# Ten ssm_k blocks in the head, their writes on GpSimd behind the gathers, weights ahead of them, bfloat16 one-hots

## The chip, the cores and the metric

The kernel runs on one core of a Trainium2 chip. The metric is the device time of one execution in microseconds; the median of several runs is quoted. TensorE is called PE (its weight loads PEld), VectorE DVE, ScalarE ACT, GpSimd POOL and SyncE SP. A DMA is issued on the queue of an engine: SP, ACT or POOL.

## The reference

Two branches work on the same tokens, `x = A_q` of 2048 rows by 512 columns, and a gate mixes them:

```python
g = _sigmoid((x * gate_w).sum(-1, keepdims=True))
a = _A_ref(x, A_k, A_v, A_shift_k, A_ssm_k, A_ssm_D, B_x, ...)   # abridged
b = _B_ref(x, B_w_router, B_w_gate, B_w_up, B_w_down)
return g * a + (1 - g) * b
```

`a` is a short causal convolution of k (4 taps), times v, then a long causal convolution along the 2048 tokens with `ssm_k` (an FFT per channel in the reference), times q. `b` is a mixture of 8 experts: the router's logits choose two experts for each token, each expert is `(silu(x Wg) * (x Wu)) Wd` with 1376 hidden columns, and the softmax of the two logits weighs them.

## The kernel before

**The stream.** The experts are worked through one after the other, the fullest first. Expert r takes up to 568 rows, gathered from DRAM by an index list. Every matmul of an expert is done in three passes over split numbers (a high part, names ending in h, and a low part, ending in l), so that a weight tile `raw` gives `gh` (ACT) and `gl` (DVE), a down weight `rd` gives `dh` and `dl`, and the transposed tokens give `xh` (ACT) and `xl` (DVE). For one weight tile ft and one half h of the rows, `product(ft, h, u)` makes g (u = 0) and then u (u = 1) in PSUM banks of the tag "gu", of which there are three in turn; ACT's silu of g (`sg`) frees a bank, and so does DVE's multiplication of `sg` by u. The first half are token tiles 0 and 1, the second half tiles 2 to 4.

**The fill.** The long convolution is a transform in two stages. Stage 1 of `ssm_k` treats 16 blocks: a block is loaded (`k_load`, tile `kr`), PE multiplies it by a constant (`stage1_f32`, two matmuls of 512 columns in float32), the result is moved from PSUM to SBUF and written to the DRAM tensor `kd` (`out1`). Six blocks (`SEQ_N`), ks1 to ks6, are done in the head, ahead of expert 0. The other ten are generators that are stepped between the products of the experts (`tick`), as are the later stages of the convolution.

**The head.** Up to `order.close()` the order of every engine is the order of the program text: the tokens are read transposed, the router's logits, the ranks, the counts per expert, then for the first expert the index list: one-hots `hots` on DVE, small matmuls `list` on PE, `idf` and `gidx` on DVE, and five gathers `xg` on POOL. The number of the first expert, `eor0`, has to be read by SP before it can load that expert's weights. Each gathered tile is transposed on PE (`xgp`), giving `xh` and `xl`. `busy` issues matmuls with no use for their result. After the head a scheduler orders the rest.

**Buffers.** Pairs of blocks lie in tiles of 1024 columns: the tag "B" has 5 of them, "ev" has 3; "A" has 6 tiles of 512 columns. A tile given out again waits for the last reader of the one before it in that place.

Of the kernel before, what the change touches and what calls it, by code (L numbers as in the profile page):

```python
# [11 lines left out]
F32 = mybir.dt.float32  # L12
# [44 lines left out]
SEQ_N = 6  # L57
BUSY = (14, 3, 4, 1, 10, 6, 6)
# [77 lines left out]
def gated_mix(ctx: ExitStack, tc: tile.TileContext, a, out):  # L136
# [113 lines left out]
    def out1(p, dst, pl, name, later=False):  # L250
# [25 lines left out]
    def stage1_f32(x, dst, pl, name, later=False):  # L276
        if ordered and pl % 2 == 0:
            p = [turned(f"{name}p{t}") for t in range(2)]
        else:
            both = banks(f"{name}p")  # L280
            p = [half(both, t) for t in range(2)]
# [8 lines left out]
        out1(p if ordered else both, dst, pl, name, later)  # L290
# [22 lines left out]
    def k_out(pl, later=False):  # L313
        stage1_f32(kr[pl], kd, pl, f"ks{pl}", later)
# [180 lines left out]
    def ticks(n):  # L495
        for _ in range(n):
            tick()

# [4 lines left out]
    def expert(r):  # L503
# [12 lines left out]
        def load(ft, eng=sync):  # L516
# [4 lines left out]
            if r == 0 and ft in QN and not ordered:  # L521
                with after("act 0"):
                    act.dma_start(raw[:, :n], src)
# [4 lines left out]
            st["raw", ft] = raw[:, :n]  # L528

# [13 lines left out]
        def product(ft, h, u, hi_first=False):  # L543
# [13 lines left out]
            for kt in range(KT):  # L557
                last = mm3(p[:fw, :nn], ghv[:, u, kt], glv[:, u, kt], xh[:, kt, sl], xl[:, kt, sl],
                           start=(kt == 0), stop=(kt == KT - 1))
            return last  # L560

        def load_down(ft, eng=sync):
# [3 lines left out]
            if r == 0 and ft in QR and not ordered:  # L566
                with after("act 0"):
                    act.dma_start(rd[:fw], src)
            else:
                eng.dma_start(rd[:fw], src)  # L570
            st["rd", ft] = rd

# [130 lines left out]
    sums = rp.tile([P, 4, P], BF16, name="sums")  # L703
    pool.memset(sums[:, 2], 1.0)
# [14 lines left out]
    sync.dma_start(late, a["c_small"][:, P:NLATE])  # L719
    k_load(k_order[3])  # L720
    k_load(k_order[4])
    with after("sp"):
        pool.dma_start(cr, a["c_r"])
    sync.dma_start(c2, a["c_r2"])

# [61 lines left out]
    k_out(k_order[0])  # L787
    k_load(k_order[5])
    k_out(k_order[1])
# [7 lines left out]
    k_out(k_order[2])  # L797
    k_out(k_order[3])
# [14 lines left out]
    dve.tensor_tensor(oh0, key, top.to_broadcast([P, E]), op=ALU.is_equal)  # L813
    s0 = rp.tile([P, PL], F32, name="s0")
    n0 = rp.tile([P, PL], F32, name="n0")
    u0 = rp.tile([P, PL], F32, name="u0")
    e0 = rp.tile([P, E], F32, name="e0")
    ef0 = rp.tile([P, 1], F32, name="ef0")
    g5 = rp.tile([P, PL, TILES], F32, name="g5")
    dve.tensor_mul(w0, w0, oh0.unsqueeze(2).to_broadcast([P, E, PL]))  # L820
    dve.tensor_mul(e0, oh0, io8)
    dve.tensor_reduce(s0, w0.rearrange("p e a -> p a e"), op=ALU.add, axis=AX.X)
    dve.tensor_reduce(ef0, e0, op=ALU.add, axis=AX.X)
    s5 = [P, PL, TILES]
    dve.tensor_tensor(g5, s0.unsqueeze(2).to_broadcast(s5), thr[:, :TILES].unsqueeze(1).to_broadcast(s5), op=ALU.is_gt)
    dve.tensor_copy(eor0, ef0)
# [62 lines left out]
    k_out(k_order[4])  # L889
    act.activation(G, L9[:, :, E], AF.Exp, scale=-1.0)  # L890
    first.split(0, act)
    busy(none, BUSY[2])
    for i in range(0, PL, 4):
        dve.tensor_tensor(hot[:, i:i + 4], u0[:, i:i + 4].unsqueeze(2).to_broadcast([P, 4, P]),
                          io128n.unsqueeze(1).to_broadcast([P, 4, P]), op=ALU.is_equal)
        for j in range(i, i + 4):
            pe.matmul(pv0, hot[:, j], val0[:, j], start=(j == 0), stop=(j == PL - 1))
        if i + 4 < PL:
            busy(none, BUSY[3])
    read(0, pv0)  # L900
    k_out(k_order[5], later=True)
# [7 lines left out]
    act.activation(z, z, AF.Exp)  # L909
    rows0 = gather(0)  # L910
    next(rows0)
# [257 lines left out]
```

## Time and profile before

| | us |
|---|---|
| median of 3 runs | 965.4 (963.39 to 966.9) |
| the profiled execution | 962.82 |
| its span, first to last instruction | 960.9 |
| PE busy in the span | 941.3 (98%) |
| DVE busy | 619.4 (64%) |
| ACT busy | 538.2 (56%) |
| POOL busy | 139.6 (15%) |

The profiled execution is 1.9 us longer than its span, and lies 2.6 us below the median. An instruction's row gives its start and its duration; rows overlap a little, since the engines are pipelined, so the distance of two starts is the better price of one in a row of many. The bracket at a row's end is the time in which the engine had nothing to do before it, and what ended that.

### The profile page before, as it was taken

The numbers are of one execution on the slowest core, as the hardware profiler recorded it, in microseconds if no ns is written. First come the engines' busy times: TensorE is split into PE (matmuls) and PEld (weight loads), VectorE is DVE, ScalarE is ACT, GpSimd is POOL, SyncE is SP. The second block draws the span as 40 slices with busy tenths as digits, with TensorE's granted clock in tenths as the row PEclk, the third lists the DMA queues.
The fourth block names the chain that finished last, engine by engine and source line by source line (L and its number), as shares of the span: only waits on it lengthen the run. The fifth ranks groups of instructions, "written<-read, shape, count | busy, mean of one in ns | idle before, by whom it ended". The sixth has DMA issues, their size and how long they took to land. (4 is left out here: it accounts for less than half of the span.)

```text
span 960.9 us, 18311 instructions
## 1 busy us (share of the span) xinstructions
PE 941.3 (98%) x7079; PEld 832.4 (87%) x7079; DVE 619.4 (64%) x1160; ACT 538.2 (56%) x881; POOL 139.6 (15%) x125
## 2 busy tenths in 40 slices
PE   8799999999999999999999999999999999999996
PEld 3589999999999999888889898888888887888895
DVE  4597689889999454745656555664676655554541
ACT  3453344454646645678667877677776672334330
POOL 1202011300103020031100301003120301020002
PEclk9899999999999999999999999999999999999998
DMA  8875875644657445474434754457453849875413
GB/s 299 308 265 195 302 244 179 174 149 168 220 179 197 145 135 187 146 183 167 143 129 161 179 170 152 128 169 182 164 165 113 207 143 315 268 197 143 116 31 44
DMA packets 78827, 171.93 MB, mean 179 GB/s; under 512 B 8625, under 2 KB 9521, under 8 KB 78610
## 3 DMA queue, kind: packets, MB, share of 16 engines
q1 hardware_dynamic: 55330, 122.57, 38.7%
q0 software_dynamic: 10976, 23.78, 12.1%
q10 hardware_dynamic: 12432, 24.38, 6.8%
q8 instruction: 57, 0.93, 0.4%
q14 instruction: 32, 0.26, 0.1%
HBM read 127.13 MB, written 43.57 MB: 178 GB/s over the span
## 5 line engine op out<-in xcount | busy, mean ns | idle before, releaser
L197 PE MATMUL g<-xh,gh 128*128 128x256 f32 (+15 forms) x700 | 202.7, 290 | 1.0 <-DVE sg L589 1.0
L197 PE MATMUL u<-xh,gh 128*128 128x256 f32 (+14 forms) x704 | 202.0, 287 | 0.7 <-ACT sg L588 0.6
L198 PE MATMUL u<-xl,gh 128*128 128x256 f32 (+14 forms) x704 | 201.6, 286 | 0.0
L199 PE MATMUL u<-xh,gl 128*128 128x256 f32 (+14 forms) x704 | 201.3, 286 | 0.0
L198 PE MATMUL g<-xl,gh 128*128 128x256 f32 (+15 forms) x700 | 200.1, 286 | 0.0
L199 PE MATMUL g<-xh,gl 128*128 128x256 f32 (+15 forms) x700 | 200.1, 286 | 0.0
L197 PEld LDWEIGHTS g<-xh,gh 128*128 128x128 f32 (+1 forms) x700 | 130.2, 186 | 16.9 <-issue 9.6
L197 PEld LDWEIGHTS u<-xh,gh 128*128 128x128 f32 (+1 forms) x704 | 130.9, 186 | 7.4 <-issue 4.0
L589 DVE TENSOR_TENSOR sg<-sg,u 128x256 f32<-128x256 f32 (+14 forms) x176 | 74.7, 425 | 95.8 <-PE u L199 84.9
L199 PEld LDWEIGHTS u<-xh,gl 128*128 128x128 f32 (+1 forms) x704 | 131.0, 186 | 5.7 <-issue 5.7
L590 ACT ACTIVATE hh<-sg 128x256 fp32r<-128x256 f32 (+14 forms) x176 | 73.5, 419 | 111.2 <-DVE sg L589 110.9
L198 PEld LDWEIGHTS u<-xl,gh 128*128 128x128 f32 (+1 forms) x704 | 131.0, 186 | 5.3 <-issue 4.9
L199 PEld LDWEIGHTS g<-xh,gl 128*128 128x128 f32 (+1 forms) x700 | 130.3, 186 | 5.9 <-issue 5.7
L198 PEld LDWEIGHTS g<-xl,gh 128*128 128x128 f32 (+1 forms) x700 | 130.2, 186 | 5.0 <-issue 3.2
L197 PE MATMUL yp<-hh,dh 128*128 128x264 f32 (+12 forms) x440 | 127.2, 291 | 0.0
L198 PE MATMUL yp<-hl,dh 128*128 128x264 f32 (+12 forms) x440 | 126.6, 289 | 0.0
L199 PE MATMUL yp<-hh,dl 128*128 128x264 f32 (+12 forms) x440 | 126.4, 289 | 0.0
L541 DVE TENSOR_TENSOR gl<-raw,gh 128x1024 fp32r<-128x1024 f32 (+2 forms) x89 | 105.4, 1184 | 22.9 <-ACT gh L535 22.2
L535 ACT ACTIVATE gh<-raw 128x1024 fp32r<-128x1024 f32 (+1 forms) x88 | 91.2, 1036 | 42.4 <-PE u L198 31.1
L588 ACT ACTIVATE sg<-g 128x256 f32<-128x256 f32 (+14 forms) x176 | 67.4, 386 | 80.8 <-PE g L199 72.2
L597 ACT ACTIVATE dh<-rd 128x512 fp32r<-128x512 f32 (+1 forms) x88 | 53.3, 627 | 70.5 <-DMA rd<-in_wd 30.6
L460 POOL DMA_INDIRECT xg<-in_q,gidx x37 | 44.7, 1207 | 325.8 <-PE xgp L469 288.7
(286 smaller groups left out, 1614.3 us busy)
## 6 DMA issues: line engine op xcount, KB each, us to landing
raw<-in_wgu SPq DMA_DIRECT2D x78, 512.0 KB
rd<-in_wd SPq DMA_DIRECT2D x77, 256.0 KB
kl<-kd SPq DMA_DIRECT2D x16, 512.0 KB
xl<-xd SPq DMA_DIRECT2D x32, 256.0 KB
zd<-ze ACTq DMA_DIRECT2D x16, 512.0 KB
zl<-zd SPq DMA_DIRECT2D x16, 512.0 KB
out<-zt SPq DMA_DIRECT2D x21, 256.0 KB
krow<-in_kpad SPq DMA_DIRECT2D x19, 256.0 KB
```

The source lines that it names most:

```text
L197: pe.matmul(p, wh, hi, start=start, stop=False)
L198: pe.matmul(p, wh, lo, start=False, stop=False)
L199: return pe.matmul(p, wl, hi, start=False, stop=stop)
L460: anchor["pool"] = pool.indirect_dma_start(out=xg[:w], out_offset=None, in_=a["q"], in_offset=bass.IndirectOffsetOnAxis(ap=gidx[:w, col:co ...
L535: act.activation(st["gh", ft], raw, AF.Copy)
L541: dve.tensor_sub(st["gl", ft][:, c], raw[:, c], st["gh", ft][:, c].bitcast(F32))
L588: act.activation(sg[:fw, :nn], pp[0][:fw, :nn], AF.Silu)
L589: dve.tensor_mul(sg[:fw, :nn], sg[:fw, :nn], pp[1][:fw, :nn])
L590: act.activation(hh[:fw, sl], sg[:fw, :nn], AF.Copy)
L597: act.activation(dh[:fw], rd[:fw], AF.Copy)
```

## The change

The head now does ten blocks of stage 1 (`SEQ_N` 10) and the stream six. All ten are loaded at the program's start, right behind the tokens and constants, and fill the five "B" places. Nothing is written to `kd` until the gathers have been issued: the writes are collected in `written` and then issued on POOL, behind the five gathers, as 13 DMAs. So the results stay in SBUF: ks1, ks3 and ks5 in "A", ks2, ks4, ks6, ks8 and ks10 in "ev", ks7 and ks9 in "B". Since "ev" has three places, ks8 takes the place of ks2, and ks10 that of ks4, when those have been written. Four of the results are moved out of PSUM later than their matmuls (`hold`), ks7, ks8 and ks10 by DVE. The last two gathered tiles move from "A" to places of the transposed tokens.

The one-hots are made from bfloat16 operands, with the four compared tokens innermost, against a table `io4` that POOL makes. The three steps from `oh0` to `eor0` go from DVE to POOL, as five. The silu table is loaded earlier on ACT, `busy` runs less, and the loads of raw2, rd0 and rd1 on ACT's queue come later.

```diff
-SEQ_N = 6
-BUSY = (14, 3, 4, 1, 10, 6, 6)
+SEQ_N = 10
+BUSY = (14, 3, 1, 6, 3)
...
-        if pl % 2:
+        both = None
+        if home == "A":
             evs = [t2k("A", 6, f"{name}e{t}") for t in range(2)]
         else:
-            both = two("ev", f"{name}e")
+            both = two(home, f"{name}e")
             evs = [half(both, t) for t in range(2)]
         for t in range(2):
-            act.activation(evs[t], p[t], AF.Copy)
-            if later:
-                written.append(lambda t=t: act.dma_start(dst[:, t, pl, :], evs[t]))
+            if eng is dve:
+                dve.tensor_copy(evs[t], p[t])
             else:
+                act.activation(evs[t], p[t], AF.Copy)
+            if not later:
                 sync.dma_start(dst[:, t, pl, :], evs[t])
+        if later and both is not None:
+            written.append(lambda: pool.dma_start(dst[:, :, pl, :], split2(both)))
+        elif later:
+            written.extend(lambda t=t: pool.dma_start(dst[:, t, pl, :], evs[t]) for t in range(2))
...
-            xg = t2k("A", 6, f"xg{r}_{n}")
+            xg = rp.tile([P, D], F32, tag="xt", bufs=XT, name=f"xg{r}_{n}")
...
+    for n in range(5, SEQ_N):
+        k_load(k_order[n])
...
+    pool.tensor_copy(io4, io128n.unsqueeze(2).to_broadcast([P, P, 4]))
...
-    u0 = rp.tile([P, PL], F32, name="u0")
+    u0 = rp.tile([P, PL], BF16, name="u0")
...
+    for h in (4, 2, 1):
+        pool.tensor_add(e0[:, :h], e0[:, :h], e0[:, h:2 * h])
+    pool.tensor_copy(eor0, e0[:, :1])
...
+    for i in range(4):
+        dve.tensor_tensor(hot0[:, i], u0[:, 4 * i:4 * i + 4].unsqueeze(1).to_broadcast([P, P, 4]), io4, op=ALU.is_equal)
...
     next(rows0)
+    k_out(k_order[6], home="B", eng=dve, later=True)
+    first.split(0, dve, halves=(0, 1))
+    evict = k_out(k_order[7], home="ev", banks_of=bank, eng=dve, later=True, hold=True)
+    busy(none, BUSY[3])
+    next(rows0)
+    evict()
+    evict = k_out(k_order[8], home="B", later=True, hold=True)
     busy(none, BUSY[4])
     next(rows0)
-    first.split(0, dve, halves=(0,))
-    busy(none, BUSY[5])
+    evict()
+    evict = k_out(k_order[9], home="ev", banks_of=turned, eng=dve, later=True, hold=True)
+    first.product(0, 0, 0, hi_first=True)
+    first.split(1, act)
+    evict()
     next(rows0)
-    first.split(0, dve, halves=(1,))
+    first.load(2, act)
+    first.load_down(0, act)
     for f in written:
         f()
```

What this does to the order of three engines, in the names of the built programs (ks8e is block ks8 in SBUF, xgp_1 the second gathered tile in PSUM; a number behind a name is an instance). DVE, from the routing's last steps to the splitting of the gathered tiles, before and then after:

```order
L908 TENSOR_TENSOR s_161<-s_161 128x16
L472 TENSOR_TENSOR xl_407<-xgp_0_428,xh_406 128x4x128
L541 TENSOR_TENSOR gl_0_435<-raw_0_346,gh_0_360 128x512
L472 TENSOR_TENSOR xl_407<-xgp_1_443,xh_406 128x4x128
L541 TENSOR_TENSOR gl_0_435<-raw_0_346,gh_0_360 128x512
L472 TENSOR_TENSOR xl_407<-xgp_2_477,xh_406 128x4x128
L541 TENSOR_TENSOR gl_1_599<-raw_1_348,gh_1_484 128x1024
```

```order
L916 TENSOR_TENSOR s_168<-s_168 128x16
L264 COPY ks7e<-ks7p 128x512 x2
L545 TENSOR_TENSOR gl_0_417<-raw_0_346,gh_0_389 128x1024
L479 TENSOR_TENSOR xl_400<-xgp_0_429,xh_399 128x4x128
L264 COPY ks8e<-ks8p_419 128x512
L264 COPY ks8e<-ks8p_420 128x512
L479 TENSOR_TENSOR xl_400<-xgp_1_445,xh_399 128x4x128
L545 TENSOR_TENSOR gl_1_613<-raw_1_348,gh_1_472 128x1024
L264 COPY ks10e<-ks10p_455 128x512
L264 COPY ks10e<-ks10p_456 128x512
L479 TENSOR_TENSOR xl_400<-xgp_2_477,xh_399 128x4x128
```

Between the low parts of the gathered tiles 0, 1 and 2 there now stand the copies of ks8 and ks10. POOL, from the gathers on, before and then after:

```order
L460 DMA xg_3_414<-in_q,gidx 128x512
L460 DMA xg_4_416<-in_q,gidx 56x512
L311 TENSOR_TENSOR kr_1681<-kr_1681,dD 1x512
L460 DMA xg_0_1348<-in_q,gidx 128x512
L460 DMA xg_1_1350<-in_q,gidx 128x512
```

```order
L467 DMA xg_3_407<-in_q,gidx 128x512
L467 DMA xg_4_409<-in_q,gidx 56x512
L272 DMA kd<-ks1e_273 128x512
L272 DMA kd<-ks1e_274 128x512
L270 DMA kd<-ks2e 256x1x512
L272 DMA kd<-ks3e_293 128x512
L272 DMA kd<-ks3e_294 128x512
L270 DMA kd<-ks4e 256x1x512
```

The write of ks2 is POOL's third behind the last gather, that of ks4 its sixth. ACT, around the first silu of expert 0 (sg_0_0) up to that of the second half (sg_0_1), before and then after:

```order
L588 ACTIVATE sg_0_0_525<-g_0_0_464 128x256
L471 ACTIVATE xh_406<-xgp_3_499 128x4x128
L471 ACTIVATE xh_406<-xgp_4_506 128x4x56
L590 ACTIVATE hh_0_523<-sg_0_0_525 128x256
L253 ACTIVATE ks7e<-ks7p 128x1024
L254 DMA kd<-ks7e 256x1x512
L597 ACTIVATE dh_0_561<-rd_0_455 128x512
L588 ACTIVATE sg_0_1_556<-g_0_1_530 128x312
```

```order
L528 DMA raw_2_484<-in_wgu 128x1024
L576 ISA
L576 DMA rd_0_486<-in_wd 128x512
L574 ISA
L574 DMA rd_1_679<-in_wd 128x512
L478 ACTIVATE xh_399<-xgp_3_514 128x4x128
L478 ACTIVATE xh_399<-xgp_4_521 128x4x56
L595 ACTIVATE sg_0_0_539<-g_0_0_459 128x256
L597 ACTIVATE hh_0_537<-sg_0_0_539 128x256
L604 ACTIVATE dh_0_575<-rd_0_486 128x512
L604 ACTIVATE dh_1_681<-rd_1_679 128x512
L595 ACTIVATE sg_0_1_570<-g_0_1_544 128x312
```

The loads of raw2, rd0 and rd1 now stand behind the third tile's high part (the row ahead of these), and the conversions dh_0 and dh_1 both stand ahead of the silu of the second half, sg_0_1; before, dh_1 stood behind it.

## Rows read from the trace of the kernel before

**Rows 1.** The table of stretches of the span: length, then busy time and instructions of PE, PEld, DVE, ACT and POOL, the granted clock of PE as a share of full speed, the busy share of the DMA engines and what they moved in GB/s. The stream, and the end.
```profile
100.00:900.00 800.00, 798.38 (x6092) 719.30 (x6089) 530.75 (x930) 480.87 (x775) 119.51 (x101) 1.00 0.59 180
900.00:960.00 60.00, 52.18 (x346) 45.59 (x345) 22.68 (x39) 13.62 (x28) 7.43 (x5) 0.95 0.26 43
```

**Rows 2.** Who made PE wait: the longest in the first 100 us, and the longest in the rest (engine, operation, line, what it waited for: us in total, times, longest).
```profile
PE xgp L469 <- DMA xg<-in_q,gidx: 5.7, 1, 5.7
...
PE g L197 <- DVE sg L589: 1.0, 1, 1.0
```

**Rows 3.** The same table of stretches as in group 1, for single microseconds around PE's longest wait.
```profile
29.00:30.00 1.00, 0.34 (x4) 0.06 (x1) 0.00 (x0) 0.00 (x0) 0.96 (x1) 1.00 0.84 199
...
32.00:33.00 1.00, 0.00 (x0) 0.00 (x0) 0.00 (x0) 0.40 (x1) 0.69 (x2) 0.87 1.05 406
...
34.00:35.00 1.00, 0.00 (x0) 0.03 (x1) 0.00 (x0) 0.74 (x3) 0.00 (x0) 0.50 1.04 418
...
39.00:40.00 1.00, 1.00 (x8) 0.93 (x7) 1.00 (x2) 0.00 (x0) 0.00 (x0) 0.72 0.86 297
```

**Rows 4.** The timeline of the routing's end (start us, us, engine, line, operation, out<-in, shapes, count, and in brackets the idle time before and its releaser): DVE and PE up to the list, then the first and the last of POOL's five gathers.
```profile
22.18 0.16 DVE L821 TENSOR_TENSOR e<-oh,rc 128x8 f32<-128x8 f32 x1
...
22.59 0.15 DVE L823 TENSOR_REDUCE ef<-e 128x1 f32<-128x8 f32 x1
...
22.86 0.15 DVE L826 CAST eor<-ef 128x1 int32<-128x1 f32 x1
...
23.94 2.49 DVE L894 TENSOR_TENSOR hots<-u,rc 128x512 bf16<-128x512 f32 x4
...
26.49 0.26 PE L897 MATMUL list<-vals,hots 128*128 128x10 bf16 x4 [0.22 <-DVE hots L894]
...
26.78 0.17 DVE L866 TENSOR_SCALAR idf<-list 128x5 f32<-128x5 f32 x1 [0.35 <-PE list L897]
...
27.18 0.17 DVE L869 TENSOR_SCALAR gidx<-idf 128x5 int32<-128x5 f32 x1
...
27.63 1.06 POOL L460 DMA_INDIRECT xg<-in_q,gidx  x1 [10.31 <-DVE gidx L869]
...
32.78 0.93 POOL L460 DMA_INDIRECT xg<-in_q,gidx  x1 [0.30 <-issue]
```

**Rows 5.** DVE's instructions by line and shape in the first 180 us (busy us, mean ns of one): a two-input operation in bfloat16 throughout, the one-hots themselves, one of half their columns, and the low part of a gathered tile.
```profile
L850 DVE TENSOR_TENSOR vals<-hots,pay 128x448 bf16<-128x448 bf16 x20 | 12.4, 663 | 0.0
...
L894 DVE TENSOR_TENSOR hots<-u,rc 128x512 bf16<-128x512 f32 x4 | 2.5, 683 | 0.0
...
L764 DVE TENSOR_TENSOR gt<-L 128x256 f32<-128x256 f32 x4 | 1.9, 465 | 0.1
...
L472 DVE TENSOR_TENSOR xl<-xgp,xh 128x512 fp32r<-128x512 f32 x8 | 5.5, 686 | 11.3 <-ACT xh L471 11.2
```

**Rows 6.** POOL's instructions by line over the span: direct DMAs of 128 rows (L295) and of 256 rows (L427), a two-input operation of 128 columns, and its smallest arithmetic.
```profile
L295 POOL DMA_DIRECT2D mf<-in_c_mf x16 | 9.9, 617 | 76.0 <-PE x2p L368 55.4 <-PE g L199 14.6 <-PE xgp L469 6.1
...
L427 POOL DMA_DIRECT2D out<-ye x8 | 9.8, 1225 | 109.5 <-DVE ye L425 103.8 <-DMA out<-ya,sidx 5.7
...
L785 POOL TENSOR_TENSOR before<-before,ident 128x128 f32<-128x128 f32 x1 | 0.5, 453 | 0.1
...
L1160 POOL MEMSET const-float32-1.0<- 128x1 f32 x1 | 0.1, 101 | 0.0
```

**Rows 7.** The timelines of the issuing queues of SP and ACT around the wait and after it.
```profile
23.86 1.85 SPq L266 DMA_DIRECT2D kd<-ks4e  x2
...
26.85 0.90 SPq L525 DMA_DIRECT2D raw<-in_wgu  x2
...
38.88 1.51 SPq L221 DMA_DIRECT2D kr<-in_ssk  x3
...
39.93 0.40 ACTq L570 DMA_DIRECT2D rd<-in_wd  x1
...
48.42 0.34 ACTq L568 DMA_DIRECT2D rd<-in_wd  x1
```

**Rows 8.** ACT's timeline: instructions that waited for a transfer of group 7 (raw0, rd0 and rd2 by their order on the queues).
```profile
32.60 1.06 ACT L535 ACTIVATE gh<-raw 128x1024 fp32r<-128x1024 f32 x1 [6.84 <-DMA raw<-in_wgu]
...
46.91 0.63 ACT L597 ACTIVATE dh<-rd 128x512 fp32r<-128x512 f32 x1 [0.68 <-DMA rd<-in_wd]
...
51.74 0.63 ACT L597 ACTIVATE dh<-rd 128x512 fp32r<-128x512 f32 x1 [0.58 <-DMA rd<-in_wd]
```

**Rows 9.** PE's timeline from the first transposed tile into the stream of expert 0; the two last rows are one block of stage 1 in the stream and what follows it.
```profile
35.00 1.08 PE L469 MATMUL xgp<-ident,xg 128*128 128x128 f32 x4 [5.66 <-DMA xg<-in_q,gidx]
...
39.15 0.90 PE L555 MATMUL g<-xh,gh 128*128 128x256 f32 x4
...
40.37 0.64 PE L555 MATMUL g<-xl,gh 128*128 128x256 f32 x4
...
42.71 0.98 PE L469 MATMUL xgp<-ident,xg 128*128 128x128 f32 x8
...
44.55 0.41 PE L197 MATMUL g<-xh,gh 128*128 128x312 f32 x1
...
49.69 1.13 PE L286 MATMUL ks8p<-kr,c 64*128 64x512 f32 x4
...
50.74 0.39 PE L197 MATMUL u<-xh,gh 128*128 128x256 f32 x1
```

More of the change, by code (lines that the diff above doesn't have):

```diff
@@ L247, in gated_mix, with out1 @@
     written = []
[L250 removed]
+    def out1(p, dst, pl, name, later=False, home=None, eng=None):
         if not ordered:
@@ L273, in stage1, with stage1_f32 @@
         out1(p, dst, pl, name)
-    def stage1_f32(x, dst, pl, name, later=False):
-        if ordered and pl % 2 == 0:
-            p = [turned(f"{name}p{t}") for t in range(2)]
+    def stage1_f32(x, dst, pl, name, later=False, home=None, eng=None, banks_of=None, hold=False):
+        if ordered and banks_of is not None:
+            p = [banks_of(f"{name}p{t}") for t in range(2)]
         else:
@@ L289, in stage1_f32 @@
             first = i
-        out1(p if ordered else both, dst, pl, name, later)
+        evict = lambda: out1(p if ordered else both, dst, pl, name, later, home, eng)
+        return evict if hold else evict()
     def mats(src, i, tag):
@@ L559, in product @@
                            start=(kt == 0), stop=(kt == KT - 1))
+            if (r, ft, h, u) == (0, 0, 1, 1):
+                anchor["pe"] = last.ins
             return last
@@ L703, in gated_mix @@
     sums = rp.tile([P, 4, P], BF16, name="sums")
+    io4 = rp.tile([P, P, 4], BF16, name="io4")
     pool.memset(sums[:, 2], 1.0)
@@ L796, in gated_mix @@
     none = bank("none")
-    k_out(k_order[2])
-    k_out(k_order[3])
+    k_out(k_order[2], home="A", later=True)
+    k_out(k_order[3], home="ev", banks_of=turned, later=True)
     cnt = cn_ps[:, :E]
@@ L888, in gated_mix @@
         first.load(ft)
-    k_out(k_order[4])
+    k_out(k_order[4], home="A", later=True)
     act.activation(G, L9[:, :, E], AF.Exp, scale=-1.0)
-    first.split(0, act)
[L892 to L901, printed above, removed]
+    busy(none, BUSY[2])
+    hot0 = hots[:, :PL * P].rearrange("p (i c j) -> p i c j", i=4, j=4)
+    for i in range(4):
+        dve.tensor_tensor(hot0[:, i], u0[:, 4 * i:4 * i + 4].unsqueeze(1).to_broadcast([P, P, 4]), io4, op=ALU.is_equal)
+        for j in range(4):
+            n = 4 * i + j
+            pe.matmul(pv0, hot0[:, i, :, j], val0[:, n], start=(n == 0), stop=(n == PL - 1))
+    read(0, pv0)
+    k_out(k_order[5], home="ev", banks_of=turned, later=True)
+    first.split(0, act)
     dve.tensor_copy(mi0[:, :E], key)
@@ L909, in gated_mix @@
     act.activation(z, z, AF.Exp)
+    act.activation(sg0, key[:, :1], AF.Silu)
     rows0 = gather(0)
     next(rows0)
+    k_out(k_order[6], home="B", eng=dve, later=True)
[5 more added lines that the diff above has]
+    evict = k_out(k_order[8], home="B", later=True, hold=True)
     busy(none, BUSY[4])
     next(rows0)
-    first.split(0, dve, halves=(0,))
-    busy(none, BUSY[5])
+    evict()
[3 more added lines that the diff above has]
+    evict()
     next(rows0)
-    first.split(0, dve, halves=(1,))
+    first.load(2, act)
+    first.load_down(0, act)
     for f in written:
         f()
-    first.load(2, act)
-    first.load_down(0, act)
-    act.activation(sg0, key[:, :1], AF.Silu)
-    busy(none, BUSY[6])
-    first.product(0, 0, 0, hi_first=True)
-    next(rows0)
-    first.split(1, act)
-    anchor["pe"] = first.product(0, 0, 1).ins
+    first.product(0, 0, 1)
     for _ in range(RM - 3):
```

32 lines of the change are left out of this document (13 added, 19 removed).

## The prediction

> **What bounds the kernel now.** I read the table of stretches first. From 100 us to 900 us PE is busy 798.4 of 800 us at full clock, and its longest wait there is 1.0 us [rows 1, 2]. So in the stream nothing counts but PE's own work: a microsecond of matmuls taken out is a microsecond gained, and work of DVE, ACT or the DMA queues that moves there costs nothing as long as PE finds its operands. Second, the list of PE's waits: one of them stands out, 5.7 us for the first gathered tile [rows 2], from 29.34 us to the transposition at 35.00 [rows 3, 9]. It has a second price: during the wait, in the microsecond from 32 on, the granted clock goes from its upper level (2.4 GHz) to the lower (1.2 GHz), and it is back only in the one from 39 on [rows 3], so PE's first 4.6 us of work behind the wait run at half speed. During the wait the DMA engines move over 400 GB/s: the gathers stand in a line of transfers. The end of the span, behind the last matmul, is not touched.
>
> The profiled execution took 962.8 us, its span 960.9; the median is 965.4. I work with differences to the profiled one and add them to the median.
>
> **Work that leaves the stream.** Four blocks more are done in the head. One block in the stream costs 1.05 us from its start to that of the next matmul, with a row of 1.13 [rows 9]; I take 1.1. I use the first matmul of the second half, at 44.55 us [rows 9], as the milestone; ks7 lies ahead of it before, so three blocks behind it go: **3.3 us gained**. The work of the ten blocks in the head, 1.13 us each, stands where PE had `busy` or nothing, so it costs nothing while the wait lasts.
>
> **How early the gathers start.** `gidx` is ready at 27.35 us [rows 4]. Three small steps leave DVE ahead of it, 0.15 to 0.16 us each with some overlap: 0.4 us. The four one-hots take 2.49 us [rows 4]. No row shows a packed bfloat16 operation: the nearest, all bfloat16 but with one operand repeated innermost, takes 663 ns for 448 columns, no faster per column than float32's 683 for 512; if the new form took as long as half the columns, it would be like the 465 ns of 256 columns [rows 5]. So 0 to 0.87 us; the new form repeats nothing innermost, which the nearest row does, and I take half, 0.45. `gidx` comes at 26.5 (26.1 to 26.95). The Trainium skill, "VectorE: DVE Perf Modes", "What auto-detection actually checks", says that an operation whose tensors are all 16 bit with step 1 does two elements a cycle; by that it would be an estimated 1.0 us instead of 0.45, and the total 0.5 us less.
>
> The number of the first expert now takes five small POOL operations, 0.1 to 0.45 us each [rows 6], from 22.2 us on: 22.7 to 24.5. SP issued the weights 1.1 us after its last write of ks4 [rows 7], so they go out at 23.8 to 25.6 instead of 26.85. The split of raw0 stays off the path.
>
> The five gathers take POOL from 27.63 to 33.71, 6.1 us, 0.28 us after `gidx` [rows 4]: now 26.8 to 32.9. The first tile lay 7.4 us between issue and use [rows 4, 9]; the 1 MB of writes of ks4 and ks5 on SP's queue around the weights is gone [rows 7], at 418 GB/s [rows 3] 2.5 us: use at 31.7, and up to 1 us sooner for the earlier weights. Take 31. PE is kept busy until about 30 by ks6 to ks8. Transposition and high part take 0.6 us each at full clock, ks9 and three `busy` 1.5, so the second tile's high part is there at about 34.3, and the eight matmuls of the first product that need only high parts end at about **35.3**, where they stood at 40.37 before [rows 9]. That much of the change works.
>
> **The wait that takes its place.** The last four matmuls of that product need the low part of tile 1, and DVE has the copies of ks8 ahead of it. ks8 lies in the place of ks2, so DVE waits until ks2 has been written, and that write is POOL's third behind the gathers. 32.9, plus two DMAs of 128 rows at 0.6 us [rows 6], gives an issue at 34.1. How long it takes to land no row shows for POOL. From below: rd2 was used 3.3 us after its issue; from above: raw0, behind writes, 5.75 us [rows 7, 8]. That is 37.4 to 39.85. I take 39.1, near the upper end: from 34 on the DMA engines have 1 MB of ks1 and ks2 to write, and 1 MB of later blocks, which SP issues as soon as the second high part is there (38.88 before [rows 7]); 2.1 MB at 418 GB/s is 5 us. Two copies of 512 columns and the low part, at 0.65 to 0.69 us each [rows 5], follow: PE goes on at **41.1**, against 40.37 before. Queued behind DVE's wait are the low parts of tiles 1 to 4 and of the second weight tile; PE waits for all of them.
>
> The Trainium skill, "DMA: Bandwidth & Descriptors", "Anatomy of one DMA — SWDGE (gpsimd) path", puts one DMA issued from GpSimd at 2.0 us plus its bytes at 436 GB/s, for 512 KB an estimated 3.2 us; by that it lands at 37.3 and the total is 1.8 us less. The rows show more than that where transfers queue (5.75 us).
>
> **The clock.** PE then has waited 5.8 us, as long as before, so I take the clock to fall as before, and the same 4.6 us at half speed to follow. Before, `busy` filled most of these; now the product does. From 40.37 to 42.71 PE did the rest of that product, one transposition and u in 2.34 us [rows 9]; at half speed 4.7, to 45.8. The last two transpositions take 0.8, then ACT makes two high parts and the silu, about 1.0: the milestone is at **47.6** instead of 44.55, 3.05 us lost.
>
> **Sum:** +3.05 - 3.3 = -0.25 us: 962.6 against 962.8 profiled, 965.1 as a median, 965 rounded. With the write landing at 37.4 and `gidx` at 26.1 it is -0.25 - 1.7 - 0.4, with 39.85 and 26.95 it is -0.25 + 0.75 + 0.45: 963.0 to 966.3.
>
> **The rivals.**
> - *The write lands soon enough for the clock.* If ks2 is written a little below the lower bound, at 36.8, PE waits 3.5 us instead of 5.7, and I take it to keep its clock. Then 38.8 + 2.34 + 0.8 + 1.0 = 42.9, 1.6 us ahead of the milestone: -4.9, **960.5**. For it: the DMA engines have slack between the gathers. Against: 2.7 us from issue is less than any row.
> - *DVE doesn't wait.* If the copies of ks8 found their place free, 35.3 + 2.34 + 0.8 + 1.0 = 39.4: -8.4, **957**. Against it stands the order of POOL's queue.
> - *Slower: the down weights stand behind the writes.* ACT now issues raw2, rd0 and rd1 only at about 43.7 to 45, behind ks5 to ks10, 3.1 MB or 7.5 us of writes, and it converts both rd0 and rd1 ahead of the silu of the second half. Before, rd0 was used 7.0 us after its issue [rows 7, 8]. The bank of that silu is wanted by the second product of the next tile, at about 47.6 + 3.3 + 1.4 = 52.3. If rd1 lands later than about 51.3, PE stops for each further microsecond; at 54 to 55 that is some 3.5 us on top: **968.5**. For it: the backlog; against: ACT's queue need not wait for POOL's.
>
> **How the numbers follow.** A measurement of this kernel tells about 0.3%, 2.9 us, from no change. The forecast, 965, has 0.50; the write in time 0.18; no wait 0.07; the late down weights 0.25. So faster by over 0.3% 0.25, within it 0.50, slower 0.25. The range leaves out the no-wait case and little of the last: 960 to 969.
>
> **What would show it.** Right: DVE's first copy of ks8 preceded by an idle time released by a DMA on kd, from about 33 to 39 us; PE idle from about 35 to 41 with the low part of tile 1 as releaser; the clock at half from about 39 to 45; PE without a longer wait behind 48; six blocks of stage 1 in the stream instead of ten. Wrong: if DVE's copies of ks8 start before 36 us, or if PE waits behind 50 us on the silu of the second half. If the hots take under 1.5 us, the bfloat16 form does two columns at a time.

## The result, and the profile after

| | before | after |
|---|---|---|
| median, us | 965.4 | 973.38 |
| the runs, us | 963.39 to 966.9 | 969.63, 970.01, 973.38, 974.29, 974.58 |
| ratio to before, 95% interval | | 1.0080 (1.0055 to 1.0105) |
| the profiled execution and its span, us | 962.82 and 960.9 | 969.63 and 967.7 |

The changed kernel is slower by 0.8%, about 8 us, where 965 with a range of 960 to 969 was forecast. The profiled execution is the shortest of the five, so its trace shows the loss at its smallest, 6.8 us.

The routing and the start of the gathers first: the number of the first expert on POOL, the one-hots and `gidx` on DVE, the weights on SP, the first gather and the write of ks2 on POOL (the timelines of the changed kernel).

```profile
23.23 0.19 POOL L831 CAST eor<-e 128x1 int32<-128x1 f32 x1
...
23.99 1.42 DVE L903 TENSOR_TENSOR hots<-u,io 128x512 bf16<-128x512 bf16 x4
...
26.20 0.17 DVE L878 TENSOR_SCALAR gidx<-idf 128x5 int32<-128x5 f32 x1
...
24.44 0.91 SPq L528 DMA_DIRECT2D raw<-in_wgu  x2
...
26.64 1.08 POOL L467 DMA_INDIRECT xg<-in_q,gidx  x1 [3.23 <-DVE gidx L878]
...
33.94 0.72 POOL L270 DMA_DIRECT2D kd<-ks2e  x1
```

Against [rows 4, 7]: the four one-hots take 1.42 instead of 2.49 us, `gidx` comes 5.00 us behind the step `key` (at 21.20) where it came 6.00 us behind it (at 21.18), and the weights go out at 24.44 instead of 26.85. PE's timeline in the same execution:

```profile
30.33 0.63 PE L476 MATMUL xgp<-ident,xg 128*128 128x128 f32 x4 [1.03 <-DMA xg<-in_q,gidx]
...
34.75 0.64 PE L559 MATMUL g<-xh,gl 128*128 128x256 f32 x4
...
42.57 1.22 PE L559 MATMUL g<-xl,gh 128*128 128x256 f32 x4 [7.18 <-DVE xl L479]
...
48.99 0.41 PE L197 MATMUL g<-xh,gh 128*128 128x312 f32 x1 [0.54 <-ACT xh L478]
...
57.13 0.39 PE L197 MATMUL u<-xh,gh 128*128 128x256 f32 x1 [2.54 <-ACT sg L595]
```

The first transposition starts at 30.33 (35.00 before, [rows 9]), and the eight matmuls that need high parts alone end at 34.75 + 0.64, about 35.4. Then PE stands for 7.2 us. The list of PE's longest waits (us in total, times, longest) and DVE's timeline name the cause:

```profile
PE g L559 <- DVE xl L479: 7.2, 1, 7.2
...
PE u L197 <- ACT sg L595: 3.9, 2, 2.5
```

```profile
40.63 1.29 DVE L264 COPY ks8e<-ks8p 128x512 f32<-128x512 f32 x2 [8.31 <-DMA kd<-ks2e]
...
41.83 0.68 DVE L479 TENSOR_TENSOR xl<-xgp,xh 128x512 fp32r<-128x512 f32 x1
```

The wait for the first tile has shrunk from 5.7 us [rows 2] to 1.03, and in its place there is one for a low part: DVE's copy of ks8 waits for the write of ks2, issued at 33.94. The issue table gives us from issue to landing (the last number):

```profile
rd<-in_wd ACTq DMA_DIRECT2D x3, 256.0 KB, 9.4
...
kd<-ks2e POOLq DMA_DIRECT2D x1, 512.0 KB, 6.7
```

A second loss stands behind the milestone, the first matmul of the second half (48.99 instead of 44.55). ACT's timeline there:

```profile
45.44 1.12 ACTq L576 DMA_DIRECT2D rd<-in_wd  x1
...
46.74 1.12 ACTq L574 DMA_DIRECT2D rd<-in_wd  x1
...
55.13 0.63 ACT L604 ACTIVATE dh<-rd 128x512 fp32r<-128x512 f32 x1 [3.89 <-DMA rd<-in_wd]
...
56.13 0.63 ACT L604 ACTIVATE dh<-rd 128x512 fp32r<-128x512 f32 x1 [0.37 <-DMA rd<-in_wd]
...
56.66 0.41 ACT L595 ACTIVATE sg<-g 128x312 f32<-128x312 f32 x1
```

ACT issues rd0 and rd1 at 45.4 to 47.9 and then stands 3.89 us for rd0; sg_0_1 stands behind both conversions, so PE waits 2.54 us for its bank, to 57.13. (The list's other wait for a silu, 1.4 us, stands far behind, between 300 and 400 us.) The table of stretches for single microseconds (columns as in group 1) shows what PE's clock does, and when the line of transfers is empty:

```profile
38.00:39.00 1.00, 0.00 (x0) 0.00 (x0) 0.00 (x0) 0.00 (x0) 0.83 (x2) 0.50 1.04 369
...
47.00:48.00 1.00, 1.00 (x6) 0.67 (x5) 0.14 (x1) 0.00 (x0) 0.52 (x1) 0.50 1.03 418
...
55.00:56.00 1.00, 0.00 (x0) 0.00 (x0) 0.21 (x1) 0.63 (x1) 0.00 (x0) 1.00 0.12 45
...
60.00:61.00 1.00, 1.00 (x4) 0.00 (x0) 1.00 (x6) 0.00 (x0) 0.00 (x0) 0.50 0.91 268
```

The clock is at its lower level from 38 to 48 us, with PE at work from 42.57 on, and again around 60, behind the second wait. The DMA engines are full up to 54 us and nearly empty at 55. Finally the same table from the milestone to 100 us, for before and then for after (with 100 to 900 us; before's is in [rows 1]):

```profile
44.55:100.00 55.45, 55.18 (x455) 49.28 (x454) 46.60 (x132) 27.47 (x49) 5.26 (x4) 1.00 0.65 224
```

```profile
48.99:100.00 51.01, 48.13 (x367) 42.03 (x368) 45.66 (x129) 22.27 (x39) 5.99 (x4) 0.97 0.65 223
100.00:900.00 800.00, 797.63 (x6119) 722.07 (x6118) 528.12 (x927) 482.45 (x779) 121.35 (x100) 1.00 0.58 177
```

From such rows every kernel below can be split in four. Idle is length less PE's busy time from the milestone to 900 us. What half speed costs is (1 - granted clock) times the length up to 100 us, an estimate. The rest is span less all of these: PE's own work behind the milestone.

| us | milestone | idle | half speed | rest | span |
|---|---|---|---|---|---|
| before | 44.55 | 1.9 | 0 | 914.5 | 960.9 |
| after | 48.99 | 5.25 | 1.5 | 912.0 | 967.7 |
| e2 (loads early) | 51.82 | 0.9 | 0 | 910.9 | 963.6 |
| e15 (silu first) | 51.62 | 2.3 | 0 | 911.1 | 965.0 |
| e1 (free places) | 42.03 | 4.2 | 1.7 | 911.2 | 959.1 |
| e5 (best) | 40.10 | 3.8 | 1.8 | 910.4 | 956.1 |

After against before: +4.4 (milestone), +3.4 (idle), +1.5 (half speed), -2.5 (work) = +6.8 us. Of the 3.4 us of idleness 2.6 lie ahead of 100 us (51.01 - 48.13 against 55.45 - 55.18) and 0.8 in the stream behind. All five kernels of the table with ten blocks in the head have a rest of 910.4 to 912.0; they differ in the other columns. Each row is one execution: those of after and e15 are the shortest of their kernel, those of e1 and e5 the longest, so the rows lie nearer together than the medians below.

### The profile page after: what moved, and what is told of

The parts are those of the page before. It is cut to its first block, busy times and chain, and to the rows that moved or that the text cites. A ratio compares the mean times of both kernels' runs of the same rounds, so it can differ in the third digit from the quotient of the medians.

```text
span 967.7 us, 18294 instructions
## 1 busy us (share of the span) xinstructions
PE 941.6 (97%) x7060; PEld 833.0 (86%) x7060; DVE 621.8 (64%) x1162; ACT 536.8 (55%) x879; POOL 153.5 (16%) x144
## 5 line engine op out<-in xcount | busy, mean ns | idle before, releaser
L545 DVE TENSOR_TENSOR gl<-raw,gh 128x1024 fp32r<-128x1024 f32 (+1 forms) x88 | 105.3, 1196 | 19.6 <-ACT gh L539 18.7
L598 DVE TENSOR_TENSOR hl<-sg,hh 128x256 fp32r<-128x256 f32 (+14 forms) x176 | 75.0, 428 | 30.2 <-ACT hh L597 29.6
```

Source lines behind the costliest of these rows:

```text
L545: dve.tensor_sub(st["gl", ft][:, c], raw[:, c], st["gh", ft][:, c].bitcast(F32))
L598: dve.tensor_sub(hl[:fw, sl], sg[:fw, :nn], hh[:fw, sl].bitcast(F32))
```

## The experiments

Theory: DVE's wait for the write of ks2 (a place given out again too soon) holds PE, and the loads of raw2, rd0 and rd1, which ACT issues only behind PE's third transposition, come late and hold it a second time. First rival: the backlog of transfers itself costs it, and the places are only where it shows. Each edit is to the changed kernel unless another is named. The times, with the runs of before made beside them:

| | median | before | ratio, 95% interval |
|---|---|---|---|
| e1 free places | 959.32 | 963.91 | 0.9947 (0.9930 to 0.9965) |
| e2 loads early | 965.92 | 963.91 | 1.0013 (1.0002 to 1.0025) |
| e3 both | 959.18 | 963.91 | 0.9945 (0.9925 to 0.9964) |
| e4 routing only (on before) | 964.34 | 963.91 | 1.0000 (0.9985 to 1.0014) |
| e5 both, kr behind the last tile | 956.53 | 964.53 | 0.9917 (0.9903 to 0.9931) |
| e6 useless matmuls on the path | 970.61 | 964.53 | 1.0069 (1.0055 to 1.0083) |
| e7 ks2 and ks4 first | 967.86 | 964.53 | 1.0026 (1.0013 to 1.0039) |
| e8 kr behind the last tile | 968.04 | 964.53 | 1.0038 (1.0024 to 1.0051) |
| e9 both, kr behind the third tile | 957.06 | 963.79 | 0.9928 (0.9916 to 0.9940) |
| e10 as e5, blocks later | 958.82 | 963.79 | 0.9948 (0.9935 to 0.9961) |
| e11 useless matmuls in the wait | 966.88 | 963.79 | 1.0028 (1.0018 to 1.0038) |
| e12 after again | 970.77 | 963.79 | 1.0075 (1.0061 to 1.0089) |
| e13 free place for ks8 alone | 963.68 | 964.45 | 0.9988 (0.9977 to 0.9998) |
| e14 as e11 | 966.22 | 964.45 | 1.0013 (1.0003 to 1.0022) |
| e15 silu first | 969.63 | 964.40 | 1.0061 (1.0047 to 1.0075) |

**e1, free places.**

```diff
+        elif home == "F":
+            evs = [t2k(("fh", "fl")[t], FX, f"{name}e{t}") for t in range(2)]
...
-    evict = k_out(k_order[7], home="ev", banks_of=bank, eng=dve, later=True, hold=True)
+    evict = k_out(k_order[7], home="F", banks_of=bank, eng=dve, later=True, hold=True)
...
-    evict = k_out(k_order[9], home="ev", banks_of=turned, eng=dve, later=True, hold=True)
+    evict = k_out(k_order[9], home="F", banks_of=turned, eng=dve, later=True, hold=True)
```

> The changed kernel, but ks8 and ks10 get places in SBUF that nothing has used (the tags fh and fl, first wanted by the stage of x in the stream), so that DVE's copies wait for no write. Theory (place wait and late loads): the 7.2 us of PE's wait for the low part go to under 2 us, the clock stays up, and the first matmul of the second half comes at about 42 instead of 48.99; the loads of raw2, rd0 and rd1 still stand behind the writes, so up to 3 us of PE's wait for the silu of the second half stay: 963 to 967 us. Rival (the backlog of transfers itself costs it, the place is only where it shows): PE waits as long between 35 and 50 us for something else, and the time stays at 969 to 974.

PE's timeline of e1: the last four matmuls of the first product, now without a wait, the milestone, and the longest wait that is left.

```profile
36.63 0.64 PE L561 MATMUL g<-xl,gh 128*128 128x256 f32 x4
...
42.03 0.41 PE L197 MATMUL g<-xh,gh 128*128 128x312 f32 x1 [2.08 <-ACT xh L480]
...
64.10 0.41 PE L197 MATMUL u<-xh,gh 128*128 128x312 f32 x1 [3.27 <-DVE sg L598]
```

0.9947 against 1.0080: the edit takes 1.3%, some 12.5 us, and turns the change into a gain, more than the 963 to 967 expected. The product runs through without a wait, although the same 5 MB of writes are issued on the same queue. The first rival falls: the backlog alone does not cost it (that it sets the length of the wait, e7 and e8 show). What stays is a wait of 2.08 us ahead of the milestone, since ACT issues the loads between two high parts, and one of 3.27 us at 64 us, behind late loads. In e1 the scheduler also put the silu of the second half ahead of dh_0 and dh_1, which e15 prices by itself, with DVE's wait still there.

**e2, loads early.**

```diff
     evict()
+    first.load(2, act)
+    first.load_down(0, act)
+    first.load_down(1, act)
     evict = k_out(k_order[8], home="B", later=True, hold=True)
...
-    first.load(2, act)
-    first.load_down(0, act)
     for f in written:
```

> The changed kernel, but ACT issues the loads of raw2, rd0 and rd1 behind the second tile's high part, ahead of the writes in time; the places are as in the changed kernel. Theory (place wait and late loads are two separate costs): PE's wait of 7.2 us stays, and is 1 to 2 us longer, since 1 MB more goes ahead of the write of ks2; the waits of PE for the silu of the second half (3.9 us in all) and the clock's second fall go, 5 to 6 us less: 967 to 971. Rival (the second wait is only the first one, passed on): the wait for the silu stays at 2 us or more, and the time at 972 to 976.

Timelines of e2, PE and then ACT, and the table of stretches from its milestone to 100 us:

```profile
45.73 1.23 PE L559 MATMUL g<-xl,gh 128*128 128x256 f32 x4 [10.31 <-DVE xl L479]
...
51.92 1.16 ACT L604 ACTIVATE dh<-rd 128x512 fp32r<-128x512 f32 x2
...
54.47 0.43 ACT L595 ACTIVATE sg<-g 128x312 f32<-128x312 f32 x1 [0.40 <-PE g L199]
...
51.82:100.00 48.18, 47.88 (x373) 41.77 (x374) 45.78 (x129) 22.87 (x40) 9.80 (x4) 1.00 0.63 220
```

The wait for the low part grew by 3.1 us, more than expected, and still the time fell by 0.6 to 0.7%, to a little below the 967 expected. dh_0 and dh_1 stand ahead of the silu as in the changed kernel, but no longer wait, and PE's waits and half speed behind the milestone are gone (0.9 and 0 in the table). So the second loss can be taken away while the first stays.

**e3, both**, and **e5, e9, e10**, with both edits and SP's loads of kr for the stream moved back. What e5 adds to e3 (e9 has it at `(0, QA)`, the third tile; e10 has three empty steps ahead of ks11 as well):

```diff
-        if (r, n) == (0, 1):
-            anchor["act 1"] = i.ins
...
         if (r, n) == (0, RA):
+            anchor["act 1"] = i.ins
```

> Both edits together: free places for ks8 and ks10 and the three loads ahead of the writes. Theory: no wait of PE above 2 us behind 36 us and the clock up from there on: four blocks less in the stream and a milestone at 41 to 43 give 957 to 963, under the kernel before. Rival (backlog): 967 or more.

> Free places for ks8 and ks10 and early loads of raw2, rd0 and rd1, and beside that SP's loads of kr for the stream (1 MB) are issued behind the high part of the last gathered tile instead of behind that of the second. With both edits but not this one, the gathered tiles 3 and 4 came 1.1 and 0.3 us late and the clock fell for a few microseconds, some 2 to 3 us in all. Theory (the transfers between 31 and 40 us share the DMA engines with the last gathers): without the 1 MB those waits go, 956 to 958. Rival (the loads of raw2, rd0 and rd1 alone delay the gathers): as with both edits, 959 to 960.

> Free places, early loads, and SP's loads of kr behind the high part of the third gathered tile (between the two places tried so far: behind that of the second, and behind that of the last). With them behind the last, the block ks11 waited 3.1 us for its load and the clock fell behind that; with them behind the second, the gathered tiles 3 and 4 were late. Theory (the 1 MB can stand where neither is wanted): neither wait, no fall of the clock behind 36 us, 952 to 955. Rival (the transfers between 32 and 50 us fill the engines, whoever comes first makes another wait): 956 to 959.

> Free places, early loads, kr behind the last gathered tile, and the first block of the stream, ks11, three steps later (ahead of the second half of weight tile 3 instead of tile 1), so that its load has some 20 us more. Theory: the wait of 3.1 us and the half clock behind it (about 2 us) go and nothing takes their place: 951.5 to 954. Rival (the weights of tiles 2 and 3 wait in the same line): 955.5 to 957.5.

PE's timelines of e3 and e5, with the wait that is new in each:

```profile
39.18 0.63 PE L478 MATMUL xgp<-ident,xg 128*128 128x128 f32 x4 [1.08 <-DMA xg<-in_q,gidx]
```

```profile
49.92 1.13 PE L294 MATMUL ks11p<-kr,c 64*128 64x512 f32 x4 [3.14 <-DMA kr<-in_ssk]
```

Both edits together gain no more than the free places alone: the early loads take 1.1 us from the gathered tile 3. With 1 MB of kr moved away from there (e5) another 0.3% comes, and ks11 waits 3.14 us for it; in e9 a wait of 1.98 us stands at 63 us; in e10 dh_2 waits 5.33 us for its load, and PE twice for the silu, 2.5 us in all. e5 came as its theory expected (956 to 958). e9's rival holds, and e10 is worse still than its own: each of these moves in the line of transfers made another wait elsewhere. e5, 0.83% under the kernel before, is the best version found; e9's interval overlaps with its.

**e7 and e8, where the write of ks2 stands in the line.**

```diff
-    for f in written:
+    for f in (written[2], written[5], *written[:2], *written[3:5], *written[6:]):
```

> The changed kernel with the writes of ks2 and ks4 first in POOL's line behind the gathers instead of third and sixth. Theory (the wait is the landing of these two writes): ks2 is issued 1.2 us sooner with 0.5 MB less in front, and lands 1.2 to 2.4 us sooner; ks4 2.5 us or more sooner; milestone at 46 to 47.8 and, since the loads on ACT are issued as much sooner but have as many bytes in front, 970 to 973. Rival (DVE's wait is set by the other transfers, loads of kr and weights, not by the place in POOL's line): the copies of ks8 start within 0.5 us of 40.6, as before the edit.

> The changed kernel with SP's loads of kr for the stream (1 MB, issued at 33.84 beside the writes) held back to the high part of the last gathered tile. Theory (bytes in the line): the write of ks2 has up to 1 MB less beside it and lands 1 to 2.4 us sooner, ACT's later loads have the 1 MB beside them instead: 971 to 973. Rival (the DMAs of POOL's queue take their time by themselves): the write of ks2 takes 6.7 us from issue to landing as before, and the time stays.

The issue of the write and DVE's copy of ks8, in e7 and then in e8 (the edit of e5 alone):

```profile
34.17 0.81 POOL L270 DMA_DIRECT2D kd<-ks2e  x1
...
38.86 1.29 DVE L264 COPY ks8e<-ks8p 128x512 f32<-128x512 f32 x2 [5.35 <-DMA kd<-ks2e]
```

```profile
34.93 0.72 POOL L270 DMA_DIRECT2D kd<-ks2e  x1
...
38.96 1.29 DVE L264 COPY ks8e<-ks8p 128x512 f32<-128x512 f32 x2 [6.77 <-DMA kd<-ks2e]
```

From issue to copy 4.7 and 4.0 us, where it was 6.7 (7.5 and 8.6 in e12 and e15). In both the write goes out ahead of the 1 MB of kr: in the changed kernel SP issues the first of these loads at 33.84, just ahead of the write, in e7 at 34.74, behind it, and in e8 at 47.18. In e6, where the write keeps its third place and the loads come at 35.54, 0.8 us behind it, it took 5.0. So the 1 MB of kr counts; what the place in POOL's line gives beyond coming ahead of kr is not shown. The gains, 0.4 to 0.5%, are larger than expected. In e7 the scheduler also put the silu first (e15), so a part of its gain is not the write's, and its profiled execution (964.1) is the shortest of twelve that reach from 964.1 to 969.1.

**e13, one free place** (the first two parts of e1's edit).

> The changed kernel with a free place for ks8 alone; ks10 is then the fourth block in the three places and waits for the write of ks2 (instead of ks4). In DVE's order the low part of tile 1 and the second weight tile's are then ahead of any wait; behind it stand the low parts of tiles 2 to 4, which PE wants only for the second half. Theory (what costs is the position of the wait ahead of tile 1's low part): PE finishes the first product and u without a wait, and waits 1 to 3 us at the second half, if at all; 959 to 963. Rival (any wait of DVE for a write costs the same): 966 or more.

```profile
43.23 1.29 DVE L266 COPY ks10e<-ks10p 128x512 f32<-128x512 f32 x2 [8.31 <-DMA kd<-ks2e]
...
43.98 1.72 PE L478 MATMUL xgp<-ident,xg 128*128 128x128 f32 x8 [5.90 <-DVE ks10e L266]
```

DVE's wait now stands behind the low part of tile 1, and PE (last row) waits 5.90 us all the same: the transposition of tile 3 wants the PSUM bank from which DVE has not yet copied ks10. 963.7 lies between the two forecasts: it is not only the low part that the wait holds, any bank or tile behind DVE's order is.

**e6, e11 and e14, useless matmuls.** The edit of e11 and e14; e6 has 60, in a bank of the tag "y".

```diff
+                    if i == 2 * KT and between:
+                        between()
...
+    more = half(banks("more"), 0)
-    first.product(0, 0, 0, hi_first=True)
+    first.product(0, 0, 0, hi_first=True, between=lambda: busy(more, 46))
```

> The changed kernel with 60 useless matmuls of 256 columns in a bank of their own between the eighth and the ninth matmul of the first product, that is where PE waits 7.2 us: they fill 6 to 6.5 us of the wait and take nothing from the path. Theory of the clock: PE's idleness brings the clock down; with the wait filled the clock stays up, the rest of g, u and the transpositions take 2.2 to 2.8 us less, and the first matmul of the second half comes at 46.2 to 47 instead of 48.99. If the late down weights then set the end by themselves (their issue hangs on the write of ks4, not on PE's speed), PE waits as much longer for the silu of the second half: the time stays within 1.5 us of the changed kernel's 973.4. If they do not: 970.5 to 971.5. Rival on the clock (it falls for another reason): half speed stays and nothing moves.

> The changed kernel with 46 useless matmuls of 256 columns between the eighth and the ninth matmul of the first product, in a bank that is free then (in the earlier trial of this the bank was that of the second tile's transposition, so they waited for the same low part and stood on PE's path for 8.4 us, and yet the time was no longer). They fill some 6.4 of the 7.2 us of the wait. Theory of the clock: full speed behind the wait, milestone at 46.2 to 47 instead of 48.99. Theory of the late loads (rd0 lands at 55 whatever PE does, and sets the end by itself): the gain at the milestone is given back in the wait for the silu: 971 to 974. Without that: 969.5 to 971.

> The changed kernel with 46 useless matmuls in the free bank once more: the run that was profiled (970.0) was the longest of its eight (965.3 to 967.5 the others), with a write of ks2 that took 10.5 us from its first wait instead of 8 to 9, and so could not show the clock. Theory of the clock: in a run near the median (966.9) the clock stays up from 41 us on, and PE's second half starts 2 us or more sooner than in the changed kernel. Rival: the clock falls as in the profiled run, and the gain comes from elsewhere.

PE's timelines of e6 and of e14, and one microsecond of e14's table of stretches:

```profile
41.72 8.38 PE L763 MATMUL more<-sums 128*128 128x256 bf16 x60 [4.56 <-DVE xl L479]
...
53.80 0.41 PE L197 MATMUL g<-xh,gh 128*128 128x312 f32 x1 [0.55 <-ACT xh L478]
```

```profile
35.26 5.20 PE L763 MATMUL more<-sums 128*128 128x256 bf16 x46
...
45.20 0.89 PE L561 MATMUL g<-xl,gh 128*128 128x256 f32 x4 [4.74 <-DVE xl L479]
...
51.24 0.41 PE L197 MATMUL g<-xh,gh 128*128 128x312 f32 x1 [1.07 <-ACT xh L478]
```

```profile
46.00:47.00 1.00, 1.00 (x7) 1.00 (x6) 1.00 (x3) 0.02 (x1) 0.25 (x1) 0.50 1.02 418
```

e6 missed its aim: the bank was that of tile 1's transposition, so the 8.4 us of useless work stand behind the low part, on the path. The milestone moves to 53.80, and the time is that of the changed kernel (1.0069 against 1.0075 and 1.0080). What the head lost came back behind it: idle 0.6 us from there to 900 instead of 5.25. Here too the scheduler put the silu first, and the profiled execution (967.3) is the shortest of its five, 3.3 us under the median, so how much the useless work cost by itself is not shown. In e14 the matmuls fill 5.2 us of the wait, 4.74 us of idleness are left, and the clock falls none the less, to 0.50 at 46 us. The milestone comes later than in the changed kernel, not sooner, and yet e11 and e14 are 0.5 to 0.7% shorter. Little of e14's gain is the clock's: ahead of the milestone PE works at half speed for 3.4 us instead of 5.4, an estimated 1 us, and behind it the clock falls again as in the changed kernel. In both the scheduler put the silu first, which is worth less than their gain (e15). Where the rest of it comes from stays open, all the more since both profiled executions (970.0 and 967.3) are the longest of their kernel, and a price of the clock by itself could not be shown.

**e15, silu first.**

```diff
-                act.activation(sg[:fw, :nn], pp[0][:fw, :nn], AF.Silu)
+                i = act.activation(sg[:fw, :nn], pp[0][:fw, :nn], AF.Silu)
+                if (r, ft, h) == (0, 0, 1):
+                    anchor['sg'] = i.ins
...
-            act.activation(dh[:fw], rd[:fw], AF.Copy)
+            with tc.issue_after(anchor['sg']) if (r, ft) in ((0, 0), (0, 1)) else nullcontext():
+                act.activation(dh[:fw], rd[:fw], AF.Copy)
```

> The changed kernel with one thing moved on ACT: the conversions dh_0 and dh_1 stand behind the silu of the second half, sg_0_1, instead of ahead of it. Places, loads and writes are as in the changed kernel. In four of the earlier trials (the free places, the useless matmuls, the order of the writes, ks8 alone) the scheduler made that order by itself, in the changed kernel it did not, so it is mixed into their times. Theory of the late down weights (ACT stands still for rd0 and with it the silu, whose bank PE wants): DVE's wait and PE's 7 to 8 us stay, the wait for the silu (2.5 and 1.4 us) and the clock's second fall behind it go: 3 to 5 us less than the changed kernel beside a kernel before of 964, that is 966 to 968. Rival (the weights themselves come late, whatever ACT converts first): PE waits for raw2 or the down weights instead, and the time stays at 970 to 972.

Timelines of e15, PE and then ACT:

```profile
45.15 1.22 PE L559 MATMUL g<-xl,gh 128*128 128x256 f32 x4 [9.28 <-DVE xl L479]
...
51.62 0.41 PE L197 MATMUL g<-xh,gh 128*128 128x312 f32 x1 [0.45 <-ACT xh L478]
...
54.22 0.43 ACT L595 ACTIVATE sg<-g 128x312 f32<-128x312 f32 x1 [0.40 <-PE g L199]
...
55.74 1.28 ACT L607 ACTIVATE dh<-rd 128x512 fp32r<-128x512 f32 x2 [1.08 <-DMA rd<-in_wd]
```

sg_0_1 runs at 54.22, ahead of the conversions, and PE's wait for it and the half speed behind the milestone are gone. The ratio falls by 0.14 to 0.19% only, about as much as its interval leaves uncertain, and the time lies between theory and rival: in the profiled execution the write of ks2 came later, and the milestone with it, at 51.62. That execution (967.3) is the shortest of its five. The theory also counted on 1.4 us of PE's waits that stand behind 300 us in the changed kernel and have nothing to do with these weights.

**e12, after again**, and **e4, the routing alone.** e4 is the kernel before with `io4`, the bfloat16 one-hots and the POOL steps of the change.

> The changed kernel once more, beside the other three. Its first five times lay in two groups, 969.6 and 970.0, and 973.4 to 974.6, and only one of the lower was profiled. If the groups belong to the kernel, they come again; if they were chance of the start (the first step of the routing began between 21.2 and 22.9 us in the profiled runs of these kernels), the times spread over 2 to 3 us without a gap. Theory (place wait and late loads): 971 to 974 again.

> The kernel before with only the routing's part of the change: bfloat16 one-hots against io4 and the number of the first expert on POOL. The writes of the six blocks stand as before. The index list is ready 1.2 to 1.5 us sooner. If the first gathered tile goes by its issue, PE's wait at it ends as much sooner: 964.0 to 964.5. If it goes by the line of transfers (1 MB of writes and 1 MB of weights around it), it comes no sooner and the time stays within 0.5 us of 965.4.

```profile
41.35 1.29 DVE L264 COPY ks8e<-ks8p 128x512 f32<-128x512 f32 x2 [9.12 <-DMA kd<-ks2e]
...
49.62 0.41 PE L197 MATMUL g<-xh,gh 128*128 128x312 f32 x1 [1.39 <-ACT xh L478]
```

e12 repeats the loss, 969.4 to 974.0 in six runs, four of them between the two groups of the first five, so the groups did not come again as such; the median, 970.8, is a little under the 971 to 974 expected. In its profile the milestone is at 49.62, and instead of the wait for the silu there is half speed from 50.1 to 53.5 us. In e4 (SP's queue, then PE):

```profile
29.17 0.72 SPq L525 DMA_DIRECT2D raw<-in_wgu  x2
...
32.66 1.08 PE L469 MATMUL xgp<-ident,xg 128*128 128x128 f32 x4 [2.96 <-DMA xg<-in_q,gidx]
...
45.39 1.58 PE L286 MATMUL ks7p<-kr,c 64*128 64x512 f32 x4 [2.86 <-DMA kr<-in_ssk]
```

The wait for the first tile falls to 2.96 us (5.7 in [rows 2]), but the time stays: the weights go out at 29.17, behind the writes on SP's queue, and a block waits 2.86 us for its kr at 45.39. So here the routing's gain did not reach the end; that it would with the writes moved out of the way is argued from this trace, that of one of the longer executions (966.9), and no run shows it alone.

## Why the prediction was wrong

**Work that leaves the stream: right.** 3.3 us forecast; the rest column falls from 914.5 to between 910.4 and 912.0, 2.5 in the changed kernel and up to 4.1 in e5.

**How early the gathers start: right, the one-hots undersized.** They save 1.07 us where 0.45 was taken, and 0.87 was the upper bound; `gidx` at 26.20 lies within its own (26.1 to 26.95). The Trainium skill, "VectorE: DVE Perf Modes", "What auto-detection actually checks", gave an estimated 1.0 us, and the trace agrees with it. The first eight matmuls end at 35.4, forecast was 35.3.

**The wait that takes its place: found, and mis-sized.** The write was issued at 33.94 (34.1 forecast) and took 6.7 us instead of 5.0; in e12 and e15 it took 7.5 and 8.6, and DVE's copy starts at 41.35 and 43.21. So PE went on at 42.57 instead of 41.1, and the milestone came at 48.99 instead of 47.6: the 1.4 us between them are all this term's. The forecast's upper bound, 39.85, came from a weight load; no row of before had a write in such company. e6, e7 and e8 show the larger part of this price: where ACT issues its loads late, the write took 4.0 to 5.0 us when it went out ahead of SP's 1 MB of kr, and 6.7 to 8.6 when it went out behind it. The Trainium skill, "DMA: Bandwidth & Descriptors", "Anatomy of one DMA — SWDGE (gpsimd) path", gives an estimated 3.2 us for this write; the runs show 4.0 in e8 and 6.7 in the changed kernel, so the measurement stands against it where the line is full.

**The clock: the size right, its cause not shown.** PE worked 5.4 us at half speed (4.6 forecast). But e14 shows the clock falling with 4.7 us of idleness too. The first rival took a wait of 3.5 us to leave the clock up; no run has such a wait there, but in e7 the clock fell (0.65 in the microsecond from 38 on) with PE idle only since 36.3.

**"PE without a longer wait behind 48": this step failed.** The forecast gave the late down weights 0.25 and 3.5 us. They came: the conversions start at 55.13 and 56.13, a little behind the 54 to 55 that the rival named, PE waits 2.54 us for the silu, and the clock falls a second time, which the rival did not have. Idleness and half speed together are 4.9 us beyond before; 4.1 of these lie ahead of 100 us, where these loads act, and 0.8 in the stream. e2 takes the wait away by the loads, e15 by ACT's order. So the forecast summed -3.3 and +3.05 as if PE's lateness ended at the milestone; measured they are -2.5 and +4.4, and 4.9 more. The first is a cause of the second, and the rival's own working has it so (loads issued at 43.7 to 45, behind PE's restart; measured 44.84 to 47.9): the wait for ks2 also holds ACT's queue behind the third tile. The sum counted the one and left the other at nothing.

**The price of the rival without DVE's wait: too high.** It was put at 8.4 us less than before; made so, e1 has 4.6, and its milestone comes at 42.03 instead of 39.4. That e5 has 8.0 takes two more edits, which the rival did not have, so the nearness of the two numbers is chance.

**What stays open:** why the changed kernel's eleven runs spread over 5.2 us (its two profiled ones start the step `key` at 21.20 and 21.12; in the other kernels it starts at up to 22.90, which would explain less than half), and the part of e11's and e14's gain that ACT's order does not explain.

## What to carry to other kernels

When results are kept in SBUF to be written later, count the places: each place given out again is a wait for a write, on the engine that copies, and everything behind it in that engine's order pays, PSUM banks too. Two free tiles of a tag that is first wanted later turned a loss of 0.8% into a gain of 0.5% (with the silu's order changed too). Loads that an engine issues in order behind such a wait come late as well, so issue them ahead of the bulk of the writes (e2; without DVE's wait this gained nothing more, e3), and let nothing that PE waits for stand behind a conversion of freshly loaded data.

## What the runs showed of the hardware

- A second fall of the clock followed on 2.5 us of idleness in the changed kernel, on 1.4 us in e12 and on 1.1 us in e14. A fall showed only later: at the first one PE stood from 35.4 us, and the clock was at 0.50 from 38; in e14 PE stood from 40.5 to 45.2, and it fell at 45.6, with PE at work again.
- A write of 512 KB from POOL's queue took from 4.0 us (e8, from its issue to DVE's copy) over 6.7 (after) to 8.6 (e15); where ACT issues its loads late, it took at most 5.0 (e6) ahead of SP's 1 MB of kr, and at least 6.7 behind it. In the changed kernel this moved over 400 GB/s from 40 to 48 us.
- With 8.4 us of useless matmuls on PE's path (e6) the time was that of the changed kernel; in its trace the milestone came 4.8 us later and PE then stood for 0.6 us instead of 5.25, with the silu put first. That the transfers behind caught up meanwhile is argued, not shown.
